# A fused attention, MLP and expert kernel: the zero fills of the slot table get a small tile of their own and a slot in the plan each, and the rows of expert 0 are loaded later in the load queue

## The chip, the cores and the metric

The kernel runs on one core of one Trainium2 chip. The metric is device time in microseconds (us) of one execution; lower is better. The median of three executions of the kernel before is 712.17 us (711.56 to 714.05). The trace comes from one more execution, taken by the hardware profiler. Its five engines are TensorE (PE; its weight loads are listed as PEld), VectorE (DVE), ScalarE (ACT), GpSimd (POOL) and SyncE (SP). SP and POOL both start DMA transfers; those of POOL are on a queue of their own.

## The reference, cut to what matters

```python
x = attention(q, k, v)          # 4 batches, 8 heads, 576 positions, window of 64
x = x.transpose(...).reshape(2304, 512)
h = x @ w_in                    # 512 -> 2048
g = h * tanh(softplus(h))
x = g @ w_out                   # 2048 -> 512
do_compute = x @ w_skip > 0     # tokens that go to an expert
e = argmax(x @ w_gate)          # one of 8 experts each, with its softmax weight
out = x;  out[do_compute] += gate * (relu(x @ w1[e]) @ w2[e])
```

## The kernel before, in words

**Slots.** The tokens are routed through a table in device memory, `xg_d`: 8 experts times 256 slots, 2,048 rows of 514 words (512 of the token, its gate, its token number). The row of a slot that no token takes must hold zeros and a token number out of bounds. So the kernel first fills the table (`fill_zero`, `fill_store`, tasks `fz` and `fs`), then scatters each routed token into its slot by an indirect DMA from POOL (`scatter`, tasks `sd`, lines 275 to 281), and later loads the rows of each expert (`base_load`, task `bl`, lines 1052 to 1056, for expert 0, whose last tokens are picked by matmuls; `xg_load` for the rest).

**Stages.** The first program part runs attention and the MLP over 6 blocks `m` of 384 tokens. Each block has 16 chunks of the hidden width. For chunk `c` = 16 m + f, `L1` (line 737) makes the pre-activation in a PSUM tile `ph` (ring of 2), a chain on ACT and DVE (`mn` L742, `me`, `n`, `ln`, `r` on ACT, `g` L764, `gH`, `gL` L773) makes the activation, and `L2` (line 788) adds the chunk to three output tiles `po`. Attention for the next block (`S`, `mx`, `ex`, `nm`, `PT`, `Pe`, `PV`, by pairs of heads `pr`) runs between the chunks. After 16 chunks `x_evac` (`xe`, lines 826 to 834) copies each `po` into a tile `xs`, routing works on it, and the scatter sends it. The second program part runs the 8 experts.

**Weights.** In block 0 the weights of `L2` are whole float32 words (`w_f32`). From block 1 on they are split in two halves: `wide_back` (`wb`, line 681) copies `w_f32` by a DMA on SP into a `ca` tile, `wide_H` (`wH`, line 314/316) rounds it, and `wide_L` (`wL`, line 697) takes the remainder. There are 16 such copies. The `ca` tiles are a ring of 2. Expert weights come near the end of the first part through staging tiles `st` in the ring `cv` of 2 (`expert_load`, line 330; `expert_H`, line 314/316; `expert_L`, line 340, on POOL or DVE).

**Order.** A planner (class `Plan`) orders all tasks before the program is written. It simulates a clock with an assumed cost for each task, waits for the tasks named in `after` plus a latency `lat`, for a free buffer of each ring in `get`, and for the earliest start `t0`; among the ready tasks it takes the one due first. The program is emitted in that order. On the chip each engine runs its own instructions in that order and waits only for data and buffers. Nothing of the planner's clock is left in the program. `chunk_time(c)` is the planner's time of chunk c: 32.22 + 5.11 for each of the first 16 chunks + 4.4 for each later one, so 93.5 for chunk 12, 118.4 for 17, 122.8 for 18 and 131.6 for 20.

The zero tile `zt` of the kernel before is one of the three `xs` tiles: `xsp.tile([128, XW], F32, tag="xs", name="zt")`. It is in use until all 16 stores of it are done. POOL also writes small pads into tiles that SP loads, at the place of their load task: zeros in `rk` (line 475, with the load `lqk` of a pair) and in `vt` (line 400, with the load `lv`), and the token numbers into `xs` (line 834, with `xe`). Such a pad waits until the buffer is free.

Of the kernel before, what the change touches and what calls it, by code (L numbers as in the profile page):

```python
# [9 lines left out]
F32 = mybir.dt.float32  # L10
F32R = mybir.dt.float32r
BF16 = mybir.dt.bfloat16
I32 = mybir.dt.int32
# [7 lines left out]
BIG = 65536.0  # L21
CAP = 256
# [7 lines left out]
GAP, FILL = 0.15, 0.8  # L30
E2B = 0.3
X0 = 2.6
PRICE3 = dict(P=0, V=0.0, A=0.12, G=0.2, S=0)
AHEAD = 18
EARLY = 8
# [134 lines left out]
def tile_kernel(  # L170
# [14 lines left out]
    V, A, G, PE, SP = nc.vector, nc.scalar, nc.gpsimd, nc.tensor, nc.sync  # L185
    B, H, S, D = q.shape
    NT, DM = out.shape
    DFF = w_in.shape[1]
    NE, _, F2 = w1.shape
# [5 lines left out]
    XW = DM + 2  # L195
# [4 lines left out]
    xg_d = dram.tile([NE * CAP, XW], F32, name="xg_d")  # L200
# [4 lines left out]
    xsp = wst.enter_context(tc.tile_pool(name="xsp", bufs=3))  # L205
    xtp = wst.enter_context(tc.tile_pool(name="xtp", bufs=2))

    def ctile(shape, dt, name):
        return cst.tile(shape, dt, tag=name, name=name)
# [8 lines left out]
    for p0 in (0, 64):  # L218
        sl = maskA[p0:p0 + 64]
# [33 lines left out]
    for n in (1, 1, 1, 3):  # L253
        t = ctile([128, n, NE + 1], F32, f"first{len(first_t)}")
# [11 lines left out]
    def fill_tile(zt):  # L266
        V.memset(zt[:, :DM + 1], 0.0)
        V.memset(zt[:, DM + 1:XW].bitcast(I32), int(BIG))

    def fill_store(zt, n):  # L270
        G.dma_start(out=xg_d[128 * n:128 * n + 128, :], in_=zt)
# [91 lines left out]
    T = plan.add  # L363
    VV, AA, GG, PP, SS = ("V", V), ("A", A), ("G", G), ("P", PE), ("S", SP)

    def one(eng, cost):
        return [(eng[0], eng[1], cost)]
# [7 lines left out]
    def chunk_time(c):  # L375
        m, f = divmod(c, NF)
        return T0 + (min(c, NF) * D0 + max(c - NF, 0) * D1)
# [203 lines left out]
    for pr in range(NU // 2):  # L581
        t = unit_time(2 * pr) - 5
        if pr < NPE:
            T(("lqk", pr), one(SS, 2.62 if len(runs(pr // 4)) == 1 else 5.2), lambda e, pr=pr: load_nat(pr), lat=2.3,
              get=[("rk", ("nq", pr)), ("rk", ("nk", pr))], due=t, t0=.7)
            for i in (1, 0):
                T(("nT", pr, i), one(PP, .36), lambda e, pr=pr, i=i: nat_T(pr, i), after=[("lqk", pr)] + ([("S", pr - 1)] if pr else []),
                  get=[(f"po{i}" if pr < 4 else "ps", ("tqk", pr, i))], use=[("nq", pr) if i == 0 else ("nk", pr)])
        else:
            T(("lqk", pr), one(SS, 3.6 if len(runs(pr // 4)) == 1 else 7.2), lambda e, pr=pr: load_dvt(pr), lat=2.3,  # L590
              get=[("rq", ("nq", pr)), ("rk", ("nk", pr))], due=t - 5)
        nd = sum(3 if r[3] == 0 else 2 for r in runs(pr // 4))
        T(("lv", pr), [("S", SP, .53 * nd)], lambda e, pr=pr: load_v(pr, e), lat=2.3,
          get=[("vt", ("vt", pr))], due=unit_time(2 * pr))
    for pr in range(NU // 2):
        if pr < NPE:
            T(("kT", pr), two(.52, .6), lambda e, pr=pr: nat_k(e, pr), after=[("nT", pr, 1)],
              get=[("kT", ("kT", pr))], use=[("tqk", pr, 1)], behind=[("kT", pr - 1)] * (pr > 0))
            T(("qT", pr), two(.42, .52), lambda e, pr=pr: nat_q(e, pr), after=[("nT", pr, 0)],
              get=[("qT", ("qT", pr))], use=[("tqk", pr, 0)], behind=[("qT", pr - 1)] * (pr > 0))  # L600
            pre = [("kT", pr), ("qT", pr)]
        else:
            T(("qT", pr), one(VV, 1.0), lambda e, pr=pr: dve_T(pr), after=[("lqk", pr)],
              get=[("kT", ("kT", pr)), ("qT", ("qT", pr))], use=[("nq", pr), ("nk", pr)],
# [4 lines left out]
          after=pre + ([("PT", 2 * pr + j - DEEP) for j in range(2)] if early and 2 * pr >= DEEP else []) + ([] if early else [("PT", 2 * pr - 1)]),  # L609
          get=[("ph" if early else "ps", ("sc", 2 * pr + j)) for j in range(2)],  # L610
          use=[("kT", pr), ("qT", pr)], due=unit_time(2 * pr), behind=[("S", pr - 1)] * (pr > 0))
        for j in range(2):
            u = 2 * pr + j
            T(("mx", u), one(VV, .64), lambda e, u=u: att_max(u), after=[("S", pr)], get=[("u" if u in EXTRA else "P", ("P", u))],
              use=[("sc", u)])
# [3 lines left out]
        for j in range(2):  # L619
# [3 lines left out]
              get=[("ps", ("tp", u))],  # L623
              use=[("P", u)])
            T(("Pe", u), two(.38, .47), lambda e, u=u: att_PTe(e, u), after=[("PT", u)], get=[("PT", ("PT", u))],
              use=[("tp", u)])
        T(("PV", pr), one(PP, .9), lambda e, pr=pr: att_PV(pr), after=[("Pe", 2 * pr), ("Pe", 2 * pr + 1), ("lv", pr)],
          get=[("ps", ("pv", pr))], use=[("PT", 2 * pr), ("PT", 2 * pr + 1), ("vt", pr)])
        T(("xH", pr), two(.37, .47), lambda e, pr=pr: att_xH(e, pr), after=[("PV", pr)], use=[("pv", pr)],
          get=[("xHL", ("xHL", pr // 4))] if pr % 4 == 0 else (), behind=[("xH", pr - 1)] * (pr > 0))  # L630
        if pr // 4 < WHOLE["in"]:
            continue
        T(("xL", pr), one(VV, .47), lambda e, pr=pr: att_xL(pr), after=[("xH", pr)], use=[("pv", pr)],
          due=unit_time(2 * pr) + 10)
# [64 lines left out]
    for f in range(NF):  # L699
        for kind in ("in", "out"):  # L700
# [12 lines left out]
            if n:  # L713
# [4 lines left out]
              use=[ca])  # L718
# [247 lines left out]
        def scatter(self, t):  # L966
            scatter(xs_t[self.m, self.t0 + t], self.si[:, t])

    zt = [None]

    def fill_zero():
        zt[0] = xsp.tile([128, XW], F32, tag="xs", name="zt")
        fill_tile(zt[0])

    T(("fz",), one(VV, .55), lambda e: fill_zero(), get=[("xs", "zt")], due=chunk_time(17), t0=chunk_time(17))
    for n in range(NE * CAP // 128):
        T(("fs", n), one(GG, 1.04), lambda e, n=n: fill_store(zt[0], n), after=[("fz",)], use=["zt"],
          lat=6, due=chunk_time(18) + 1.0 * n)
    T(("wg",), one(SS, 1.0), lambda e: load_wgs(), due=chunk_time(2), lat=3)

    def load_wgs():
# [4 lines left out]
    for m in range(NB):  # L986
        last = m == NB - 1
        tb = chunk_time(NC) - 8 if last else chunk_time(NF * m + NF + 2)
        dt = 0.5 if last else D1
        for t in range(3):  # L990
            T(("xe", m, t), two(.48, .6), lambda e, m=m, t=t: x_evac(e, m, t), after=[("L2t", NF * m + NF - 1, t) if last else ("L2", NF * m + NF - 1)],
              get=[("xs", ("xs", m, t))], use=[("po", m, t)], due=tb + 2)
            T(("xo", m, t), one(SS, .45), lambda e, m=m, t=t: x_store(m, t), after=[("xe", m, t)], lat=2.5,
              due=tb + 20, use=[("xs", m, t)])
            T(("rT", m, t), one(PP, .43), lambda e, m=m, t=t: route_T(m, t), after=[("xe", m, t)] + [("re", m, t - 1)] * (t > 0),
              get=[("ps", ("rtp", m, t))], due=tb + dt * (2 + 2 * t), use=[("xs", m, t)])
            T(("re", m, t), two(.48, .6), lambda e, m=m, t=t: route_Te(e, m, t), after=[("rT", m, t)],
              get=[("rk" if last else "xf", ("xf", m, t))], use=[("rtp", m, t)])
            if not last:
                T(("rl", m, t), one(PP, .25), lambda e, m=m, t=t: route_few(m, t), after=[("re", m, t), ("wg",)],  # L1000
                  get=[("ps", ("lq", m, t))], use=[("xf", m, t)], due=tb + dt * (3 + 2 * t))
                T(("rq", m, t), two(.22, .19), lambda e, m=m, t=t: route_fewe(e, m, t), after=[("rl", m, t)],
                  use=[("lq", m, t)], get=[("lqs", ("lqs", m))] if t == 0 else ())
                continue
            T(("rl", m, t), one(PP, .75), lambda e, m=m, t=t: route_lg(m, t), after=[("re", m, t), ("wg",)],
              get=[("ps", ("lp", m, t))], use=[("xf", m, t)], due=tb + dt * (3 + 2 * t))
        if not last:
            T(("rs", m), one(PP, .66), lambda e, m=m: route_sum(m), after=[("rq", m, t) for t in range(3)],
              get=[("ps", ("lp", m))], use=[("lqs", m)], due=tb + dt * 8.5)
            T(("lg", m), one(VV, .1), lambda e, m=m: route_lge(m), after=[("rs", m)], use=[("lp", m)])  # L1010
        prev = None
        for t0, n in ([(t, 1) for t in range(3)] if last else [(0, 3)]):
            g = Group(m, t0, n)
            lgs = [("lg", m) if n > 1 else ("rl", m, t0)]
            lu = [("lp", m, t0)] if n == 1 else []
            key = lambda x, m=m, t0=t0: (x, m, t0)
            td = tb + dt * 9
            gb = ("grp", m, t0)

            def R(name, eng, cost, fn, after, use=(), late=0.0, get=(), lat=None, g=g, gb=gb, td=td):  # L1020
                T(name if isinstance(name, tuple) else key(name), one(eng, cost), lambda e: fn(g), after=after,
                  use=[gb] + list(use), due=td + late, get=get, lat=lat)

            T(key("m1"), one(VV, .1), lambda e, g=g: g.max1(), after=lgs, use=lu, get=[(f"grp{n}", gb)], due=td)
            R("dm", VV, .1, Group.dm, lgs + [key("m1")], lu)
            R("su", VV, .1, Group.sub, [key("m1")], lu)
            R("se", AA, .12, Group.exp, [key("su")])
            R("fi", VV, .1, Group.first, [key("su"), key("dm")])
            R("m2", VV, .1, Group.max2, [key("fi")])
            R("oh", VV, .1, Group.onehot, [key("m2")])  # L1030
            R("pl", PP, .1, Group.place, [key("oh")] + ([prev("co")] if prev else [("co", m - 1, 0)] if m else []),
              get=[("ps", ("pp", m, t0))])
            R("pi", VV, .1, Group.pick, [key("pl")], [("pp", m, t0)], .5)
            R("ro", VV, .1, Group.row, [key("pi")], (), .5)
            R("sl", VV, .07, Group.slot, [key("ro")], (), .5)
            R("ke", VV, .07, Group.keep, [key("ro")], (), .3 if last else 6)
            R("sm", VV, .1, Group.sum, [key("se")], (), .5)
            R("ep", VV, .07, Group.eps, [key("sm")], (), .5)
            R("ga", VV, .09, Group.gate, [key("ep")], (), .5)
            R("tg", VV, .07 * n, Group.tag, [key("ga")], [("xs", m, t0 + t) for t in range(n)], .5)  # L1040
            R("co", VV, .21 * n, Group.count, [key("pl")], (), 1)
            for t in range(n):
                R(("sd", m, t0 + t), GG, 1.04, lambda g, t=t: g.scatter(t),
                  [key("sl"), key("tg"), ("xo", m, t0 + t)] + [("fs", x) for x in range(NE * CAP // 128)],
                  [("xs", m, t0 + t)], 2, lat=3)
            prev = key


# [371 lines left out]
```

## Time and profile before

| | |
|---|---|
| median of 3 executions | 712.17 us (711.56 to 714.05) |
| the profiled execution | 712.69 us |
| its span, first to last instruction | 710.9 us |
| PE busy | 685.3 us (96%) |
| DVE, ACT, POOL busy | 444.2 (62%), 396.7 (56%), 76.8 us (11%) |
| mean granted TensorE clock | 0.986 of full speed |
| chain of work that ended last | PE 76%, issue 7%, DMA 6%, DVE 4%, ACT 2% |

The chain of work that ended last is followed back from the last instruction, at each step to what released it. In the timeline rows below, the columns are start (us), length (us), engine, source line, operation, output<-input, how many were merged, and in square brackets the idle time before it with what ended it. A row that merges several instructions has the length from the first start to the last end. 1.8 us of the execution lie outside the span.

### The profile page before, as it was taken

What the parts mean: (1) busy time and instruction counts of PE and PEld (TensorE: products, weight loads), DVE (VectorE), ACT (ScalarE), POOL (GpSimd) and SP (SyncE); (2) the same over time, 40 slices, a digit from 0 to 9 for tenths busy, and PEclk for the clock granted to TensorE, in tenths of its full rate; (3) what the DMA queues carried; (4) which work ended last, traced back from release to release, by engine and by line L of the source; (5) the groups of instructions that cost most, each with busy time, mean ns of one, the idle gap of its engine ahead of it and who ended that gap; (6) DMA issues with size and microseconds to landing.
All of it is one profiled execution on the core that took longest, in us unless ns stands there. A gap on an engine that the chain in (4) does not pass through costs nothing.

```text
span 710.9 us, 13617 instructions
## 1 busy us (share of the span) xinstructions
PE 685.3 (96%) x4921; PEld 584.8 (82%) x4921; DVE 444.2 (62%) x1247; ACT 396.7 (56%) x973; POOL 76.8 (11%) x144
## 2 busy tenths in 40 slices
PE   7999999889999999999999999999988999999994
PEld 7876667678888888888888888888878998998983
DVE  5899999486566657565467556446557362574251
ACT  6778877367656675766566666556643342232120
POOL 3000000400020001000020000112232111111011
PEclk9999999989999999999999999999998999999998
DMA  7789887943213213231221200054463667788000
GB/s 176 215 242 270 263 205 158 339 153 73 42 53 87 41 29 73 46 89 30 41 54 34 64 1 9 18 184 144 131 198 105 243 237 236 265 290 290 30 24 20
DMA packets 141644, 92.53 MB, mean 130 GB/s; under 512 B 110189, under 2 KB 118381, under 8 KB 141568
## 3 DMA queue, kind: packets, MB, share of 16 engines
q1 hardware_dynamic: 137568, 82.90, 40.3%
q0 software_dynamic: 4000, 8.63, 3.4%
q8 instruction: 45, 0.74, 0.4%
q14 instruction: 31, 0.25, 0.1%
HBM read 73.96 MB, written 17.86 MB: 129 GB/s over the span
## 4 chain that ended last, share of the span: by engine, by line
PE 76%; issue 7%; DMA 6%; DVE 4%; ACT 2%; SPq 2%; POOL 1%; POOLq 0%; DVEq 0%; ACTq 0%
PE po L788 27%; PE ph L737 26%; PE ph L1209 7%; PE po L1253 4%; PE sc L508 2%; PE pv L563 2%; DMA ca<-w 2%; DMA st<-in_moe_w_dram 2%; PE tp L552 2%; DMA w<-in_moe_w_in_dram 1%; PE rtp L843 1%; DMA vt<-in_v_dram 1%; PE po L1268 1%; PE lq L857 1%; POOL out_dram L291 1%
## 5 line engine op out<-in xcount | busy, mean ns | idle before, releaser
L737 PE MATMUL ph<-xH,w 128*128 128x384 f32 x768 | 223.3, 352 | 4.3 <-DVE u L764 3.0
L788 PE MATMUL po<-w,gH 128*128 128x512 f32 x480 | 154.7, 404 | 1.8 <-ACT xs L830 1.8
L737 PEld LDWEIGHTS ph<-xH,w 128*128 128x128 f32 x768 | 141.6, 189 | 13.4 <-issue 5.1
L737 PE MATMUL ph<-xL,w 128*128 128x384 f32 x384 | 130.5, 340 | 0.0
L788 PEld LDWEIGHTS po<-w,gH 128*128 128x128 f32 x480 | 89.3, 191 | 17.2 <-ACT xs L830 2.2
L745 ACT ACTIVATE u<-u 128x384 f32<-128x384 f32 x96 | 50.0, 521 | 94.7 <-DVE u L742 94.6
L788 PE MATMUL po<-w,gL 128*128 128x512 f32 x240 | 95.8, 399 | 0.0
L764 DVE SCALAR_TENSOR_TENSOR u<-u,ph 128x384 f32<-128x384 f32 x80 | 44.1, 552 | 75.1 <-ACT u L758 74.2
L737 PEld LDWEIGHTS ph<-xL,w 128*128 128x128 f32 x384 | 72.6, 189 | 2.2 <-issue 1.4
L742 DVE TENSOR_SCALAR u<-ph 128x384 f32<-128x384 f32 x96 | 53.0, 553 | 25.9 <-PE ph L737 25.7
L531 ACT ACTIVATE P<-P,mx 128x128 f32<-128x128 f32 x144 | 55.8, 389 | 16.2 <-DVE mx L524 16.1
L1209 PEld LDWEIGHTS ph<-xgT,w 128*128 128x128 f32 x512 | 63.7, 190 | 0.9 <-ACT xgT L314 0.3
L1209 PE MATMUL ph<-xgT,w 128*128 128x144 f32 x512 | 64.1, 286 | 0.2 <-ACT xgT L314 0.2
L788 PEld LDWEIGHTS po<-w,gL 128*128 128x128 f32 x240 | 45.7, 190 | 11.6 <-DVE gL L773 0.7
L749 ACT ACTIVATE u<-u 128x384 f32<-128x384 f32 x96 | 50.3, 523 | 2.7
L755 ACT ACTIVATE u<-u 128x384 f32<-128x384 f32 x96 | 50.2, 523 | 2.6
L758 ACT ACTIVATE u<-u 128x384 f32<-128x384 f32 x96 | 50.2, 523 | 2.5
L773 DVE TENSOR_TENSOR gL<-u,gH 128x384 fp32r<-128x384 f32 x80 | 46.5, 581 | 5.9 <-ACT gH L314 3.1
L1236 ACT ACTIVATE hH<-ph 128x288 fp32r<-128x288 f32 x32 | 13.1, 410 | 60.9 <-PE ph L1209 49.9
L788 PE MATMUL po<-w,g 128*128 128x512 f32 x96 | 44.4, 599 | 0.0
L1253 PE MATMUL po<-w,hH 128*128 128x512 f32 x128 | 42.6, 414 | 0.0
L276 POOL DMA_INDIRECT xg_d<-xs,r_si x18 | 18.4, 1023 | 166.2 <-DVE P L547 78.3
(159 smaller groups left out, 1002.3 us busy)
## 6 DMA issues: line engine op xcount, KB each, us to landing
st<-in_moe_w_dram SPq DMA_DIRECT2D x64, 256.0 KB, 5.9
w<-in_moe_w_dram SPq DMA_DIRECT2D x32, 512.0 KB, 5.6
w<-in_moe_w_in_dram SPq DMA_DIRECT2D x16, 512.0 KB, 6.1
w<-in_moe_w_out_dram SPq DMA_DIRECT2D x16, 512.0 KB, 6.1
out_dram<-xs SPq DMA_DIRECT2D x18, 256.0 KB, 2.2
xg_d<-zt POOLq DMA_DIRECT2D x16, 257.0 KB, 7.1
xg<-xg_d SPq DMA_DIRECT2D x16, 257.0 KB, 3.6
ca<-w SPq DMA_DIRECT2D x16, 256.0 KB, 2.4
```

The lines of the kernel that those rows point to most:

```text
L531: A.activation(P[:, i], P[:, i], AF.Exp, bias=mx[:, 0, u % 2, i:i + 1], scale=-1.0, accum_out=mx[:, 1, u % 2, i:i + 1])
L737: PE.matmul(phs[c], a[:, kk], b[:, kk], start=kk == 0 and n == 0, stop=kk == NK - 1 and n == len(terms) - 1)
L742: V.tensor_scalar(u, phs[c], 20.0, None, op0=ALU.min)
L745: A.activation(us[c], us[c], AF.Exp)
L749: A.activation(us[c], us[c], AF.Square, bias=1.0)
L755: A.activation(us[c], us[c], AF.Ln, scale=0.5, bias=half_t[c])
L758: A.activation(us[c], us[c], AF.Exp, scale=-1.0)
L764: V.scalar_tensor_tensor(o, us[c], 1.0, phs[c], op0=ALU.subtract, op1=ALU.mult)
L773: eng.tensor_tensor(gL, us[c], gH.bitcast(F32), op=ALU.subtract)
L788: PE.matmul(po[m, t], a[:, ts], b, start=f == 0 and n == 0, stop=f == NF - 1 and n == len(terms) - 1)
L1209: PE.matmul(ph[:, i], w1_t[e, kk][:, 128 * f:128 * f + 128], xgT[e][:, kk, :N1], start=kk == 0, stop=kk == NK - 1)
L1253: PE.matmul(po2[e, s], a[:, f, ss], b, start=f == 0 and n == 0, stop=f == 7 and n == 2)
```

## The change

The zero tile is now a constant tile `nothing` of 130 words on each partition (128 zeros, one more zero, one out-of-bounds number), filled at the planner's time of chunk 12. Each of 16 stores writes the 512 token words of 128 rows from it, the 128 zeros read four times. A 17th store writes the last two words of all 2,048 rows. The stores stand in the plan from chunk 20 on, 2.5 us apart. The ring of `xs` tiles no longer holds the zero tile. And the planner's latency of a scatter goes from 3 to 6.5 us; what comes after a scatter in the plan is the load of expert 0's rows.

```diff
+FILL_AT, FILL_BY = 20, 2.5
-    zt = [None]
+    nothing = ctile([128, 1, 130], F32, "nothing")
+    NS = NE * CAP // 128
     def fill_zero():
-        zt[0] = xsp.tile([128, XW], F32, tag="xs", name="zt")
-        fill_tile(zt[0])
-    T(("fz",), one(VV, .55), lambda e: fill_zero(), get=[("xs", "zt")], due=chunk_time(17), t0=chunk_time(17))
-    for n in range(NE * CAP // 128):
-        T(("fs", n), one(GG, 1.04), lambda e, n=n: fill_store(zt[0], n), after=[("fz",)], use=["zt"],
-          lat=6, due=chunk_time(18) + 1.0 * n)
+        V.memset(nothing[:, :, :129], 0.0)
+        V.memset(nothing[:, :, 129:].bitcast(I32), int(BIG))
+    def fill_slots(n):
+        if n < NS:
+            G.dma_start(out=xg_d[128 * n:128 * n + 128, :DM].rearrange("p (a c) -> p a c", c=128),
+                        in_=nothing[:, :, :128].to_broadcast([128, DM // 128, 128]))
+        else:
+            G.dma_start(out=xg_d.rearrange("(n p) c -> p n c", p=128)[:, :, DM:XW], in_=nothing[:, :, 128:].to_broadcast([128, NS, 2]))
+    T(("fz",), one(VV, .2), lambda e: fill_zero(), due=chunk_time(12), t0=chunk_time(12))
+    for n in range(NS + 1):
+        T(("fs", n), one(GG, 1.04), lambda e, n=n: fill_slots(n), after=[("fz",)],
+          lat=6, due=chunk_time(FILL_AT) + FILL_BY * n, t0=chunk_time(FILL_AT) + FILL_BY * n)
...
                 R(("sd", m, t0 + t), GG, 1.04, lambda g, t=t: g.scatter(t),
-                  [key("sl"), key("tg"), ("xo", m, t0 + t)] + [("fs", x) for x in range(NE * CAP // 128)],
-                  [("xs", m, t0 + t)], 2, lat=3)
+                  [key("sl"), key("tg"), ("xo", m, t0 + t)] + [("fs", x) for x in range(NS + 1)],
+                  [("xs", m, t0 + t)], 2, lat=6.5)
```

## Rows read from the trace of the kernel before

**Rows 1.** Waits of PE from 60 to 560 us: total, times, longest (us).

```profile
PE sel L1062 <- DVE u L764: 3.0, 1, 3.0
PE ph L737 <- DVE u L764: 3.0, 1, 3.0
PE po L788 <- ACT xs L830: 1.8, 1, 1.8
```

**Rows 2.** Timeline of PE, 128 to 165 us.

```profile
128.43 0.42 PE L737 MATMUL ph<-xH,w 128*128 128x384 f32 x1
...
136.45 0.89 PE L508 MATMUL sc<-kT,qT 64*64 64x128 f32 x24
...
140.37 0.44 PE L737 MATMUL ph<-xH,w 128*128 128x384 f32 x1 [3.03 <-DVE u L764]
...
152.39 0.34 PE L737 MATMUL ph<-xH,w 128*128 128x384 f32 x1
...
154.51 0.64 PE L788 MATMUL po<-w,gH 128*128 128x512 f32 x2
...
156.62 0.82 PE L552 MATMUL tp<-ident,P 128*128 128x128 f32 x6
```

**Rows 3.** Windows: us, busy us (instructions) by engine, granted clock, DMA share, GB/s.

```profile
100.00:123.00 23.00, 22.70 (x130) 15.57 (x128) 22.28 (x60) 17.24 (x46) 0.16 (x1) 1.00 0.70 153
130.41:154.70 24.29, 19.48 (x116) 15.60 (x115) 15.30 (x43) 11.03 (x30) 3.29 (x9) 0.86 0.81 258
535.00:540.00 5.00, 5.00 (x25) 4.40 (x25) 1.99 (x5) 1.14 (x3) 0.29 (x1) 0.78 0.40 150
```

**Rows 4.** Timeline of DVE, 125 to 140 us.

```profile
125.08 0.55 DVE L764 SCALAR_TENSOR_TENSOR g<-u,ph 128x384 f32<-128x384 f32 x1
...
135.28 0.43 DVE L316 CAST w<-ca 128x512 fp32r<-128x512 f32 x1 [4.87 <-DMA ca<-w]
...
137.76 0.43 DVE L316 CAST w<-ca 128x512 fp32r<-128x512 f32 x1 [1.58 <-DMA ca<-w]
```

**Rows 5.** DMA from 123 to 142 us: a queue, and issues with KB and landing.

```profile
q0 software_dynamic: 1280, 4.21, 62.2%
...
ca<-w SPq DMA_DIRECT2D x4, 256.0 KB, 6.2
```

**Rows 6.** DMA issues of the whole span: KB each, median us to landing.

```profile
ca<-w SPq DMA_DIRECT2D x16, 256.0 KB, 2.4
...
wgs<-in_moe_w_skip_dram SPq DMA_DIRECT2D x1, 2.0 KB, 5.8
```

**Rows 7.** Timeline of POOL, whole span.

```profile
109.25 0.16 POOL L475 MEMSET rk<- 128x64 f32 x1 [55.28 <-DVE kT L490]
123.28 5.04 POOL L271 DMA_DIRECT2D xg_d<-zt  x9 [13.87 <-DVE mx L538]
...
162.62 0.20 POOL L400 MEMSET vt<- 64x128 f32 x1 [19.95 <-PE pv L563]
...
521.77 1.32 POOL L340 TENSOR_TENSOR w<-st,w 128x512 fp32r<-128x512 f32 x1
```

**Rows 8.** Instructions on the tile zt: ns minimum, median, maximum, first and last start.

```profile
L271 POOL DMA_DIRECT2D xg_d<-zt x16: 539/539/757, 123.3 to 134.1; - x16
```

**Rows 9.** Timeline of SP: copies of weights, expert 0's rows, staging loads.

```profile
119.20 2.00 SPq L681 DMA_DIRECT2D ca<-w  x2
...
525.27 0.89 SPq L1056 DMA_DIRECT2D base<-xg_d  x2
...
526.25 0.85 SPq L330 DMA_DIRECT2D st<-in_moe_w_dram  x2
```

**Rows 10.** The chain that ended last, in order of time, 515 to 535 us.

```profile
520.69 4.37 DMA xg_d<-xs,r_si
```

**Rows 11.** Timeline of ACT, 522 to 558 us.

```profile
530.79 0.63 ACT L314 ACTIVATE w<-st 128x512 fp32r<-128x512 f32 x1 [6.59 <-DMA st<-in_moe_w_dram]
```

**Rows 12.** Instructions on the tile xs, 200 to 240 us.

```profile
L832 DVE TENSOR_SCALAR xs<-po x1: 692/692/692, 222.2 to 222.2; 128x512 f32<-128x512 f32 x1
```

## The prediction

> **What bounds the kernel now.** I read four views in turn. The chain that ended last names TensorE for most of the span, so only time in which PE waits or runs slowly can be won. The waits of PE before the experts are few: two of 3.0 us and one of 1.8 [rows 1] (each 3.0 is one event; an earlier list by line counts it for the weight load too). So I looked at what leads to these three.
>
> *First place, 137 to 152 us.* PE ends a score group at 136.45 + 0.89 = 137.34 and is back at full pace at 152.39, 15.05 us later [rows 2]. Between them it does one L1, two L2 and four transposes. At full pace an L1 takes 154.51 - 152.39 = 2.12, an L2 156.62 - 154.51 = 2.11, and six transposes 0.82, so four 0.55 [rows 2]: 6.9 us. Lost: 15.05 - 6.9 = 8.1. A second way gives the same: waits of 3.0 + 1.8, and a granted clock of 0.86 over 24.29 us, which is 3.4 [rows 1, 3]. The cause is upstream. DVE sat idle 4.87 and 1.58 us for copies of weights `ca` [rows 4]. These took 6.2 us from issue to landing between 123 and 142, against 2.4 over the whole span, and the queue of POOL filled 62.2% of all DMA time there [rows 5, 6]. That queue carried the 16 zero stores, issued from 123.28 on, the first nine in 5.04 us [rows 7]. The 1.8 wait is the third `xs` tile, whose buffer the zero tile held.
>
> *Second place, 525 to 540 us.* SP reaches the load of expert 0's rows and must wait for the scatters, which land at 520.69 + 4.37 = 525.06 [rows 10]. It issues it at 525.27; two staging loads queued behind it go out at 526.25 [rows 9]. ACT waits 6.59 us for the first and starts at 530.79 [rows 11]; the activation chain behind it on ACT is late, and PE waits 3.0 for the `ph` buffer [rows 1]. From 535 to 540 the granted clock is 0.78, another 5 x 0.22 = 1.1 [rows 3].
>
> **The change, part by part.**
>
> *The fills leave 123 to 142.* Worth at most the 8.1. It cannot all come back. In the stretch 130.41 to 154.70 DVE is busy 15.30 us [rows 3]; with 8.1 less the stretch is 16.2, so DVE would be 94% busy and in order. I give back 1.0 (bounds 0 and 2.0, twice that).
>
> *Where they go.* The 2.5 us between stores is in the planner's clock alone. On the chip POOL runs its queue as fast as its waits allow, and its waits are few. The zero tile is ready early (planner 93.5). The pad at 109.25, for the load of pair 12, is POOL's last work before the fills, and POOL then waits 13.87 us only because the zero tile is not there [rows 7]. That wait goes. What else stands between the fills in POOL's order are pads. Following the planner of the kernel before, the load of pair 13 is at 137.2 and the v load of pair 12 at 151.9 of its clock; the fills start at 131.6 + 2.5 n. So about three come before the first of these pads, six between the two, and eight after. The pad of pair 13 needs a buffer that DVE frees some us after 109, on the same order of work as the one at 109.25. The v pad waits for a PE step that ended at 162.5 [rows 7]. So I expect about nine fills in a batch from 110 us on, and the others, with the 17th, after about 162.6 - 7 = 155.5, when the 16 copies have nearly all been issued.
>
> *Price of the first batch.* It falls on a stretch where DMA is 0.70 and DVE 22.28 of 23 us busy [rows 3]; two copies go out on SP at 119.20 [rows 9], among many small loads. Below: nothing. Nine of 16 fills would make a copy late by 9/16 of 6.2 - 2.4, which is 2.1 [rows 5, 6], and the activation that ends at 125.08 + 0.55 = 125.63 has 2.8 us until PE needs its buffer at 128.43 [rows 2, 4]. Above: 9/16 of the old 8.1, 4.6, since a DVE with 3% idle cannot make up a late start. I take 2.0, nearer to the slack, because the copies then needed are few. Of the second batch I take 0 (bounds 0 and 1.0): PE has caught up and one or two copies are left.
>
> *Smaller pieces.* A store now moves 512 pieces of 512 bytes instead of 128 rows. POOL's time for one was 539 ns at the minimum and the median [rows 8]; the bounds are that and four times that, 2.2 us. Slower would only space the batch out: cost 0. The 17th store has 2,048 pieces of 8 bytes. The nearest row is a load of 512 words that took 5.8 us [rows 6]; four times that is 23 us. It lies under the time until the first scatter is needed, below. The fill of the small tile takes DVE a fraction of what it did; a tenth or so of a us either way, taken as 0.
>
> *The later load of expert 0's rows.* In the plan the load can start 3.5 us later, so the two staging loads go ahead of it. The first needs the staging buffer that POOL frees at 521.77 + 1.32 = 523.09 [rows 7]. It is issued 526.25 - 523.1 = 3.1 earlier, ACT starts at 527.7, and the wait of 3.0 and the slow clock, 1.1, go: 4.1. The next thing late is the last chunk, whose chain follows on the same ACT and DVE: I give back 0.7. Worth 3.4, bounds 0 and 4.1. The rows of expert 0 come no later than before, for the wait on the scatters (525.06) ends their delay in either order.
>
> **The sum** is made against the profiled execution, 712.69 us; the median of the runs, 712.17, is 0.5 lower, less than any term. 712.69 - 8.1 + 1.0 + 2.0 - 3.4 = 704.2. Between the three waits and up to 560 us PE has no others of weight [rows 1], so what is won stays won.
>
> **The rivals.**
>
> *Paced.* POOL takes so long for each store that they spread out, and the first batch costs nothing: 712.69 - 8.1 + 1.0 - 3.4 = 702.2. For it: four times the pieces. Against: nine stores took 5.04 us, 0.56 each, while DVE was fully at work [rows 4, 7]. The Trainium skill ("SBUF — State Buffer", section "SBUF: two separate sides") says that POOL cannot write the descriptors of its DMAs while VectorE holds the port pair that they share. By it the stores, moved into DVE's busiest stretch, would be drawn out and the time would be this rival's 702.2; the 0.56 of those rows does not bear it out.
>
> *Stall moved.* The first batch stalls the copies of 114 to 121 us as the old one did those of 127: all of the 8.1 is given back and 712.69 - 3.4 = 709.3 is left. For it: DVE has less slack there than at 130. Against: nine fills, not 16.
>
> *No gain in the second place*, because the staging load meets another wait: 704.2 + 3.4 = 707.6.
>
> *Slower: the 17th store holds up the scatters.* The second batch starts at 155.5. At 2.2 us each its seven large stores end on POOL at 170.6, the 17th (16 times 0.54) at 179.2 and has landed, at 23.2, at 202.4. Three scatters of some 1.3 and a landing of 4.4 [rows 10] end at 210.7. The first `xs` tile of block 1 is filled at 222.2 [rows 12], after the change at some 215. So it costs nothing until the 17th store takes more than 27.6 us; at twice my figure, 46.4, it is 18.8 late, PE stands still, and the time is 704.2 + 18.8 = 723. The Trainium skill ("DMA: Bandwidth & Descriptors", section "Specifications") says that pieces under 512 bytes make the DMA read, modify and write. It speaks for this rival at 723; no row here shows a store of 8 bytes.
>
> *Reordered.* The freed ring and the new due times shift the plan around the fills; a worse order in a stretch where DVE is full takes the gain back: 710 to 716.
>
> **Chances and range.** Forecast 704.2: 0.52, its own range 701.5 to 707. Paced 0.13, stall moved 0.14, no gain in the second place 0.07, slower 0.05, reordered 0.09, of which a third ends slower. By the bounds the best is 712.69 - 8.1 - 4.1 = 700.5; above I reach past the moved stall to 710.5. That leaves out the slower rival, most of the reordered one and tails of the others, some 2 in 10. A measurement of this kernel tells 0.3%, 2.1 us, from no change. Faster by more: 0.84; within: 0.08; slower: 0.08.
>
> **What would show it.** POOL's timeline: fills from 110 us in two or three batches, split by the pads; single fills 2.5 us apart would be the pacing rival. The windows from 130 to 155: granted clock back to 1.00, no wait of DVE for `ca` of more than 1 us. DMA: copies `ca` near 2.4 us at all times but 114 to 125. SP: the rows of expert 0 behind two staging loads, ACT at its staging wait 3 us earlier, and no 3 us wait at PE's first selection matmul. I am wrong if DVE waits for copies around 117 to 125 and PE loses over 4 us there, or if a scatter waits for the 17th store.

## The result, and the profile after

The changed kernel takes 717.25 us (median of 8 runs, 716.57 to 718.15) against 712.85 us for the kernel before (8 runs, 708.86 to 714.77). The ratio is 1.0065, with a 95% interval of 1.0043 to 1.0086: slower by 0.65%, where 704.2 us, 1.2% faster, was forecast. The profiled execution took 717.19 us, with a span of 715.5.

To see where the 4.6 us between the two spans (710.9 and 715.5) went, I cut both at the same four instructions: the zeroing of the pad `rk` at 109.25 [rows 7], the first zeroing of V's pad behind the scatters, the first matmul of the experts and the last delivery. The two that have no row yet are these. Of the kernel before, the timeline of POOL and of PE:

```profile
204.88 0.20 POOL L400 MEMSET vt<- 64x128 f32 x1 [4.47 <-PE pv L563]
...
702.81 0.98 POOL L291 DMA_INDIRECT out_dram<-y,xg  x1 [5.00 <-DVEq L1388]
```

```profile
554.19 6.03 PE L1209 MATMUL ph<-xgT,w 128*128 128x144 f32 x47 [0.19 <-ACT xgT L314]
```

and of the changed kernel the same two, POOL's with the fills that answer to [rows 7]:

```profile
110.56 0.16 POOL L476 MEMSET rk<- 128x64 f32 x1 [54.50 <-DVE kT L491]
...
111.14 0.99 POOL L980 DMA_DIRECT2D xg_d<-nothing  x1 [0.18 <-issue]
...
112.37 1.54 POOL L980 DMA_DIRECT2D xg_d<-nothing  x2
...
113.98 3.21 POOL L980 DMA_DIRECT2D xg_d<-nothing  x4
119.31 0.76 POOL L980 DMA_DIRECT2D xg_d<-nothing  x1 [2.12 <-DMA rq<-in_q_dram]
168.17 0.20 POOL L401 MEMSET vt<- 64x128 f32 x1 [48.10 <-PE pv L564]
168.73 2.98 POOL L980 DMA_DIRECT2D xg_d<-nothing  x4 [0.36 <-issue]
...
181.82 1.16 POOL L983 DMA_DIRECT2D xg_d<-nothing  x1 [7.04 <-issue]
...
211.52 0.20 POOL L401 MEMSET vt<- 64x128 f32 x1 [4.55 <-PE pv L564]
...
704.80 0.98 POOL L292 DMA_INDIRECT out_dram<-y,xg  x1 [4.52 <-DVEq L1398]
```

```profile
556.63 3.58 PE L1219 MATMUL ph<-xgT,w 128*128 128x144 f32 x27 [0.20 <-ACT xgT L315]
```

| stretch, us | before | after | difference | forecast |
|---|---|---|---|---|
| span's start to the pad `rk` | 109.25 | 110.56 | +1.3 | 0 |
| to V's pad: the first place | 95.6 | 101.0 | +5.3 | -5.1 |
| to the experts: the second place | 349.3 | 345.1 | -4.2 | -3.4 |
| to the last delivery | 148.6 | 148.2 | -0.4 | 0 |
| to the end of the span | 8.1 | 10.7 | +2.6 | 0 |

Each stretch is read from one trace of each kernel. In the ten traces of this document with the new fills, the changed kernel's among them, the work up to the pad `rk` is the same, and it takes 109.0 to 113.2 us; so the +1.3 of the first line says nothing.

The second place came out as forecast. The first is off by 10.4 us, and there is a loss at the very end that I had not looked for at all.

**The first place.** POOL did what was forecast: eight stores from 111 us on, in a batch, the others behind V's pad. The old stall of PE is gone, and with it the waits of 3.0 us at `ph` and 1.8 at `po` [rows 1], but there is a larger one that begins twelve microseconds earlier, at 125.4. Its row, the longest wait of PE from 60 to 565 us, and the windows view (as in [rows 3]) of the work behind it:

```profile
134.17 0.69 PE L738 MATMUL ph<-xH,w 128*128 128x384 f32 x1 [8.79 <-DVE g L765]
```

```profile
134.17:140.07 5.90, 5.90 (x15) 4.87 (x16) 3.43 (x9) 2.83 (x6) 0.00 (x0) 0.50 0.66 157
```

So the loss has two parts. PE waits 8.8 us, and behind the wait it does 5.90 us of matmuls at a granted clock of 0.50, the lower of its two levels (1.2 GHz); at full clock these would take half, an estimate from the two levels, so 2.95 us go there. Waits of DVE from 100 to 200 us, as in [rows 1]:

```profile
DVE kT L491 <- DMA rk<-in_k_dram: 10.2, 1, 10.2
DVE w L317 <- DMA ca<-w: 7.9, 4, 6.0
```

DVE stands 10.2 us, up to 130.24, at the transpose of pair 10's keys, and PE behind it. Not a weight copy `ca` was late there but the loads of q and k. (The 6.0 us at a `ca` come later, at 177.87, behind the second batch of stores; PE then waits 0.68.) SP, which issues the loads, was itself held up. Its timeline, where most of these issues took some 0.47 us each up to 111 us:

```profile
111.36 0.42 SPq L482 DMA_DIRECT2D rk<-in_k_dram  x1
111.83 2.08 SPq L479 DMA_DIRECT2D rq<-in_q_dram  x1
...
115.59 1.21 SPq L479 DMA_DIRECT2D rq<-in_q_dram  x1
116.85 3.40 SPq L482 DMA_DIRECT2D rk<-in_k_dram  x1
120.36 8.46 SPq L411 DMA_DIRECT2D vt<-in_v_dram  x2
```

The DMA view of 110 to 130 us says with what they shared (queue: packets, MB, share of 16 engines' time; issues: KB each, median us to landing):

```profile
q0 software_dynamic: 640, 2.10, 59.1%
q1 hardware_dynamic: 6146, 1.31, 47.4%
...
xg_d<-nothing POOLq DMA_DIRECT2D x8, 256.0 KB, 9.4
...
rq<-in_q_dram SPq DMA_DIRECT2D x6, 48.0 KB, 9.4
```

Read the packets. On the mean, one of POOL's carries 2.10 MB / 640 = 3.3 KB and took 0.591 x 20 us x 16 / 640 = 0.30 us; one of SP's carries 1.31 MB / 6146 = 213 bytes. In the kernel before, POOL's packets carried as much (4.21 MB / 1280) and took 0.622 x 19 x 16 / 1280 = 0.148 us [rows 5]. So with 512-byte pieces in place of rows of 2,056 the same bytes took twice the packet time, and the packets of eight fills add up to 0.591 x 20 = 11.8 us of all sixteen engines, as those of all sixteen fills did before (0.622 x 19 = 11.8). The shares of the two queues here add up to more than 100%, so packets of different queues overlap in the record: a packet's time is not time in which its engine serves nothing else. The Trainium skill ("DMA: Bandwidth & Descriptors", section "Queues, rings and completion order") says that an engine goes round its queues by whole packets; by that a load of 128-byte pieces gives way to 3.3 KB each turn, and the landing of 9.4 us for 48 KB agrees.

**The second place.** SP issues the staging loads ahead of expert 0's rows, as was worked out from [rows 9], and ACT waits 1.42 us where it waited 6.59 [rows 11]:

```profile
528.91 2.67 SPq L331 DMA_DIRECT2D st<-in_moe_w_dram  x2
531.69 0.37 SPq L328 DMA_DIRECT2D w<-in_moe_w_dram  x1
532.36 0.88 SPq L1066 DMA_DIRECT2D base<-xg_d  x2
```

```profile
533.81 0.63 ACT L315 ACTIVATE w<-st 128x512 fp32r<-128x512 f32 x1 [1.42 <-PE ph L738]
```

The window that was at a granted clock of 0.78 [rows 3] is at full clock, and the first selection matmul does not wait:

```profile
535.00:540.00 5.00, 5.00 (x29) 4.12 (x28) 3.89 (x7) 3.57 (x8) 2.96 (x5) 1.00 0.53 173
```

**The end.** Behind the last delivery only sequencers work. POOL's last instructions belong to the closing of the program, and its longest drain (ns minimum, median, maximum) takes 2,282 ns where it took 731. First the kernel before, then the changed one:

```profile
L1415 POOLq DRAIN  x3: 44/103/731, 709.4 to 710.6; - x3
```

```profile
L1425 POOLq DRAIN  x3: 45/103/2282, 712.4 to 715.2; - x3
```

### The profile page after: what moved, and what is told of

It reads as the page before. It is cut to its first block, busy times and chain, and to the rows that moved or that the text cites. A ratio compares the mean times of both kernels' runs of the same rounds, so it can differ in the third digit from the quotient of the medians.

```text
span 715.5 us, 13609 instructions
## 1 busy us (share of the span) xinstructions
PE 684.6 (96%) x4921; PEld 583.3 (82%) x4921; DVE 444.1 (62%) x1245; ACT 397.8 (56%) x975; POOL 81.1 (11%) x145
## 5 line engine op out<-in xcount | busy, mean ns | idle before, releaser
L789 PE MATMUL po<-w,gH 128*128 128x512 f32 x480 | 152.9, 399 | 0.0
L746 ACT ACTIVATE u<-u 128x384 f32<-128x384 f32 x96 | 50.0, 521 | 89.7 <-DVE u L743 89.6
```

The costliest lines, as they stand in the source:

```text
L746: A.activation(us[c], us[c], AF.Exp)
L789: PE.matmul(po[m, t], a[:, ts], b, start=f == 0 and n == 0, stop=f == NF - 1 and n == len(terms) - 1)
```

## The experiments

In all of them the stretches of the table above are taken between the same instructions, again from one trace each. Where two kernels do the same in the first place, it differs by 0.7 us (95.6 in the kernel before, 94.9 with the later load alone) and by 1.3 (101.0 in the changed kernel, 102.3 with the fills alone). Theory A: the loss is DMA time that the early batch takes from pair 10's loads, and the second place is a separate gain. Its rivals: the loss comes from the order (the small tile is zeroed early, so the plan puts pair 10's transposes some 2.4 us earlier on DVE), or from the later load of expert 0's rows.

### One part of the change at a time

The kernel before with the later load alone:

```diff
-                  [("xs", m, t0 + t)], 2, lat=3)
+                  [("xs", m, t0 + t)], 2, lat=6.5)
```

> The kernel before with one number changed: a scatter is due to land 6.5 us after its issue instead of 3, so expert 0's rows go to the queue some 4 us later; the zero fills stay as before. Theory A (the two parts of the change are apart, and the second part gains where the forecast put it): the experts start about 4.2 us earlier than in the kernel before, and the time is 4.2 us under it, 0.9935 to 0.9950 of it. Rival (the later load's gain is given back after the last work, as the changed kernel's end, 2.2 us longer from the last delivery to the end of the span, suggests): 2.0 us under it, 0.997.

Measured: 708.86 us, 0.9938 of the kernel before (0.9910 to 0.9966). The stretch to the experts is 344.9 us against 349.3, the end 8.0. The later load is worth 4.5 us there, and nothing of it is lost at the end, so the longer end belongs to the fills.

The changed kernel without it:

```diff
-                  [("xs", m, t0 + t)], 2, lat=6.5)
+                  [("xs", m, t0 + t)], 2, lat=3)
```

> The changed kernel with the scatters' landing back at 3 us, so only the zero fills differ from the kernel before. Theory A (the batch of eight fills at 111 to 120 us costs 11.7 us against a first place without them, and 6.6 us against the kernel before): the time is 6.6 us over the kernel before, 1.008 to 1.011, and with the 2.2 us at the end, if that belongs to the fills, 1.012. Rival (the loss comes with the later load of expert 0's rows): within 0.3% of the kernel before.

Measured: 722.36 us, 1.0134 (1.0094 to 1.0174). First place 102.3 us (+6.7), second 348.4, end 10.3. The rival is out: the fills alone lose more than the whole change does, by about the 4.2 us that the other part gains.

### The same order without the early batch

In the changed kernel the stores 0 to 7 are issued where the ninth is; no other engine's order changes.

```diff
-FILL_AT, FILL_BY = 20, 2.5
+FILL_AT, FILL_BY, HOLD = 20, 2.5, 8
...
     def fill_slots(n):
+        if n < HOLD:
+            return
+        for x in range(HOLD) if n == HOLD else ():
+            fill_one(x)
+        fill_one(n)
+
+    def fill_one(n):
```

> The changed kernel with the order of every engine as it is and one difference: the first eight fills are issued together with the ninth, behind the zeroing of V's pad at 168 us, instead of at 111 to 120 us. Theory A (what was lost is DMA time: the eight fills starve pair 10's loads of q and k, and VectorE waits 10.2 us for them): that wait goes, the pads of V at 168.2 and 190.6 us come 11 to 14 us earlier, and the time is 703 to 706 us, 0.987 to 0.991 of the kernel before. Theory B (what was lost is the order: pair 10's transposes stand about 2.4 us earlier on VectorE because the small tile is zeroed early, and its loads are late with or without fills): a wait of at least 5 us stays at that transpose, and the time stays within 3 us of the changed kernel, 714 to 718 us.

Measured: 706.92 us, 0.9911 (0.9882 to 0.9941). The longest wait of PE that is left up to the experts is this:

```profile
PE ph L738 <- DVE u L765: 1.1, 1, 1.1
```

The granted clock is 1.00 from 110 to 155 us, and in the DMA view of 110 to 130 us the loads land as they should, though SP moves twice the bytes there:

```profile
q1 hardware_dynamic: 13619, 2.70, 66.1%
...
rq<-in_q_dram SPq DMA_DIRECT2D x12, 48.0 KB, 2.4
```

First place 89.7 us: 5.9 better than before, where the forecast had 5.1, and 11.3 better than the changed kernel. With the order as it was, this is theory A and against the rival of the order. The time is 1 us above the expectation; the end, 10.5 us, is still as long as in the changed kernel.

The sixteen stores now go out from 156.7 to 180 us in one row and land late (a median of 13.3 us from 155 to 182). What shares that stretch with them is late too. The loads of q and k there land in 19 us, against some 3 in the kernel before, and neither DVE nor PE waits for them: they are not needed yet. A weight copy lands late as well, and that one costs something, the price of the second batch that I had put at 0. First DVE, then PE:

```profile
166.26 0.43 DVE L317 CAST w<-ca 128x512 fp32r<-128x512 f32 x1 [6.38 <-DMA ca<-w]
```

```profile
167.93 0.44 PE L738 MATMUL ph<-xH,w 128*128 128x384 f32 x1 [1.11 <-DVE u L765]
```

### The whole row of fills later in the plan

The changed kernel with two numbers changed:

```diff
-FILL_AT, FILL_BY = 20, 2.5
+FILL_AT, FILL_BY = 25, 1.0
```

> The changed kernel with the fills planned from chunk 25 on, 1.0 us apart, instead of from chunk 20 on, 2.5 us apart: all seventeen stand behind two of the zeroings of V's and the keys' pads on POOL's queue and go out in a batch at about 155 to 172 us; SyncE's order is that of the changed kernel. Theory A: no wait for pair 10's loads, 703 to 706 us, 0.987 to 0.991 of the kernel before; a batch of seventeen there may delay what is loaded at 155 to 172 us, which would show as a VectorE wait there and cost up to the 5 us that the sixteen fills cost the kernel before. Theory B (order, not traffic): 714 to 718 us.

Measured: 707.06 us, 0.9913 (0.9882 to 0.9945). First place 90.5, second 345.4, end 10.6. The planner's own numbers do what the hold did by hand. The wait that was feared for the batch of seventeen is there, 7.2 us of DVE at a weight copy, but only 1.9 of it reach PE.

### The pace that was written, made real

In the changed kernel each store gets a small copy ahead of it that reads DVE's newest result; `recent` and the scratch tile `pace` are new:

```diff
     def m_L(eng, c):
         gH, gL = gHL[c]
+        recent[0] = gL
...
     def fill_slots(n):
+        G.tensor_copy(pace[:, n:n + 1], recent[0][:, :1].bitcast(F32))
```

> The changed kernel with a wait that paces GpSimd: in front of each of the seventeen stores it copies one column of the newest gL tile into a scratch tile, so that no store can leave before VectorE has made that gL; the order of every other engine is as in the changed kernel. Theory A (the loss is the batch at 111 to 120 us, which comes from GpSimd being ahead of the order's clock): no two stores start within 1 us of each other before 150 us, the first comes after 130 us, no VectorE wait for pair 10's loads over 1 us is left, and the time is that of the held fills, 0.988 to 0.994 of the kernel before. Rival (fills beside the loads of the attention cost what they cost, whenever they run): the waits come back a pair later, for pair 11's loads, 5 us or more, and the time is 0.997 or above.

Measured: 706.88 us, 0.9918 (0.9889 to 0.9947). Now POOL waits for DVE in front of a store, by its timeline:

```profile
130.91 0.32 POOL L981 COPY pace<-gL 128x1 f32<-128x1 f32 x1 [21.55 <-DVE gL L775]
131.17 0.99 POOL L983 DMA_DIRECT2D xg_d<-nothing  x1
...
136.00 0.18 POOL L981 COPY pace<-gL 128x1 f32<-128x1 f32 x1 [3.19 <-DVE gL L775]
136.12 0.79 POOL L983 DMA_DIRECT2D xg_d<-nothing  x1
136.90 0.20 POOL L981 COPY pace<-gL 128x1 f32<-128x1 f32 x1
137.02 0.75 POOL L983 DMA_DIRECT2D xg_d<-nothing  x1
```

The wait for pair 10's loads is gone. The pace is uneven: where a gL is already there, stores follow each other within 0.9 us, as at 136.12, so that detail of the expectation missed. PE pays 2.2 us at one gH, and the first place is 92.2 us, 2.5 worse than held; the end, 8.5 us, is 2.0 shorter. In time the two can't be told apart. The rival, a wait that returns for pair 11, did not appear.

### Half the batch

Four of the eight stay where they were; the diff is against the held kernel.

```diff
-FILL_AT, FILL_BY, HOLD = 20, 2.5, 8
+FILL_AT, FILL_BY, HOLD, NOW = 20, 2.5, 8, 4
...
-        if n < HOLD:
+        if NOW <= n < HOLD:
             return
-        for x in range(HOLD) if n == HOLD else ():
+        for x in range(NOW, HOLD) if n == HOLD else ():
```

> The changed kernel with four of the eight early fills left at 111 to 115 us and the other four held back to the ninth, behind the zeroing of V's pad. If the loss goes with the bytes that the fills put in front of pair 10's loads, VectorE's wait is about half of 10.2 us and the time about halfway between the held fills (0.991 of the kernel before) and the changed kernel (1.0065): 0.997 to 1.001. If the loads have slack for a few fills, the wait is under 1 us and the ratio 0.989 to 0.994. If the first fills alone make it, the wait stays 8 us or more and the ratio is 1.004 or more.

Measured: 710.98 us, 0.9984 (0.9962 to 1.0006). DVE's wait for pair 10's keys:

```profile
DVE kT L491 <- DMA rk<-in_k_dram: 4.5, 1, 4.5
```

No fills, four, eight: waits of 0, 4.5 and 10.2 us, first place 89.7, 94.1 and 101.0 us. DVE's wait is close to proportional, 1.1 to 1.4 us a store. In the first place the first four cost 4.4 us and the next four 6.9. The only slack seen is PE's, which is 1.4 us ahead of DVE and so waits 3.1 of the 4.5 and 8.8 of the 10.2; whether one or two stores would have fitted was not tried.

### Pieces of half the size

The changed kernel, with the early batch in its place:

```diff
-            G.dma_start(out=xg_d[128 * n:128 * n + 128, :DM].rearrange("p (a c) -> p a c", c=128),
-                        in_=nothing[:, :, :128].to_broadcast([128, DM // 128, 128]))
+            G.dma_start(out=xg_d[128 * n:128 * n + 128, :DM].rearrange("p (a c) -> p a c", c=64),
+                        in_=nothing[:, :, :64].to_broadcast([128, DM // 64, 64]))
```

> The changed kernel with each of the sixteen stores made of 1,024 pieces of 256 bytes instead of 512 pieces of 512 bytes: the same bytes at the same places of every queue, twice the pieces. If the loss in front of pair 10's loads goes with the bytes, VectorE's wait stays at 9 to 11 us and the ratio at 1.005 to 1.009; if it goes with the pieces, the wait is 15 to 20 us and the ratio 1.013 to 1.025. The end: if GpSimd's last drain goes with the pieces that it issued, the stretch from the last delivery's start to the end of the span is over 11.5 us; if it goes with the seventeenth store's 8-byte pieces alone, 10.3 to 10.7.

Measured: 734.54 us, 1.0296 (1.0271 to 1.0321). The time is above both expectations, but the wait for pair 10 is 9.6 us, not 15 to 20. The DMA view of 110 to 130 us says more:

```profile
q0 software_dynamic: 313, 1.03, 41.5%
```

Only half the bytes had gone by then, and they took 0.415 x 20 x 16 / 313 = 0.42 us a packet of the same 3.3 KB on the mean. POOL had to wait 7.89 us before its fourth store, and the rest ran on into the weight copies:

```profile
124.99 0.89 POOL L980 DMA_DIRECT2D xg_d<-nothing  x1 [7.89 <-issue]
```

```profile
DVE w L317 <- DMA ca<-w: 23.2, 4, 11.9
DVE kT L491 <- DMA rk<-in_k_dram: 9.6, 1, 9.6
```

So what counts is neither bytes nor stores alone. Counted in pieces that went out beside pair 10's loads, the three runs fall into line: 4 x 512 = 2,048 pieces and a wait of 4.5 us in the half batch, 8 x 512 = 4,096 and 10.2 us in the changed kernel, and here, up to 130 us, 1.03 MB / 256 = some 4,000 and 9.6 us. That is 2.2 to 2.5 us for each 1,000 pieces, from three runs; by that, the 8,192 pieces of all eight stores would have made some 18 to 20, as was expected, but they did not all go out in time.

The packets' times point the same way, less sharply: 0.148, 0.30 and 0.42 us a packet for pieces of 2,056, 512 and 256 bytes. These are times in a crowd, with other queues' packets between, and the crowd matters as much. At 512 bytes the DMA view gives 0.21 us in the paced run and 0.34 in the held one (both 155 to 182 us), at 256 bytes 0.34 here from 123 to 142. The Trainium skill ("DMA: Bandwidth & Descriptors", section "Specifications") puts the limit for full rate at 512 bytes; here a packet's time had already doubled at that limit, though not in the same crowd.

Two things are not told apart: the pieces' size, and that the new stores read the same few zeros over and over where the old ones read whole rows. The opposite run, rows of 2,056 bytes at the early place, was not tried.

### The end: which store it belongs to

Again against the held kernel:

```diff
-            G.dma_start(out=xg_d.rearrange("(n p) c -> p n c", p=128)[:, :, DM:XW], in_=nothing[:, :, 128:].to_broadcast([128, NS, 2]))
+            SP.dma_start(out=xg_d.rearrange("(n p) c -> p n c", p=128)[:, :, DM:XW], in_=nothing[:, :, 128:].to_broadcast([128, NS, 2]))
```

> The held fills with the seventeenth store (two words of every row, 2,048 pieces of 8 bytes) issued by SyncE instead of GpSimd. It is for the end of the program: from the last delivery's start to the end of the span the kernel before and the one with later rows alone take 8.1 and 8.0 us, every kernel with the new fills 10.3 to 10.7, with GpSimd's last drain at 2.28 us instead of 0.73. If the seventeenth store makes GpSimd's drain long, that stretch falls to 8.0 to 8.3 us and the time to about 0.988 of the kernel before; if the sixteen others do, it stays at 10.3 to 10.7 us and the ratio at 0.991.

Measured: 705.21 us, 0.9898 (0.9867 to 0.9930). POOL's longest drain falls to 894 ns, and SP issues the store in 0.47 us:

```profile
L1432 POOLq DRAIN  x3: 45/103/894, 701.6 to 703.1; - x3
```

The end is 8.8 us: 1.7 of the 2.4 us are back, less than expected. It is the seventeenth store on POOL that costs them, and not the sixteen others; in the run with twice their pieces the drain stayed at 2,282 ns and the end at 10.4 us. Which property of that store it is, its 2,048 pieces or their 8 bytes, was not tried.

Then the sixteen others as well:

```diff
-            G.dma_start(out=xg_d[128 * n:128 * n + 128, :DM].rearrange("p (a c) -> p a c", c=128),
+            SP.dma_start(out=xg_d[128 * n:128 * n + 128, :DM].rearrange("p (a c) -> p a c", c=128),
```

> The held fills with all seventeen stores issued by SyncE instead of GpSimd; nine stand in SyncE's order ahead of a wide copy and of pair 12's loads. The end: if what GpSimd issued makes its drain long, the stretch from the last delivery's start to the end of the span falls to 8.0 to 8.3 us; if not, it stays at 10.3 to 10.7. Beside it: if a store costs SyncE as much as its other issues near there (about 0.5 us), nothing is late and the time is 0.988; if the nine hold up SyncE by 1 us or more each, pair 12's loads are late, VectorE waits for them and the ratio is 0.993 or above.

Measured: 717.51 us, 1.0072 (1.0050 to 1.0094). The end is shorter than expected (6.6 us, with a longest drain of 1.13), but nine stores hold up SP for 9.60 us, and the weight copy and pair 12's loads stand behind them:

```profile
157.60 9.60 SPq L987 DMA_DIRECT2D xg_d<-nothing  x9
167.30 1.68 SPq L682 DMA_DIRECT2D ca<-w  x1
169.02 5.07 SPq L987 DMA_DIRECT2D xg_d<-nothing  x3
```

DVE waits 19.1 us at that copy and PE 13.9. The same stores on POOL's queue, at the same time, cost PE 1.1 us in the held run.

And the paced kernel with the seventeenth alone on SP:

```diff
-            G.dma_start(out=xg_d.rearrange("(n p) c -> p n c", p=128)[:, :, DM:XW], in_=nothing[:, :, 128:].to_broadcast([128, NS, 2]))
+            SP.dma_start(out=xg_d.rearrange("(n p) c -> p n c", p=128)[:, :, DM:XW], in_=nothing[:, :, 128:].to_broadcast([128, NS, 2]))
```

> The paced fills with the seventeenth store issued by SyncE. If the two gains are apart, the stretch at the end is 8.5 to 9.0 us and the ratio 0.988 to 0.991; if the pacing has cost in places that the other hid, it stays at 0.991 to 0.993.

Measured: 705.68 us, 0.9896 (0.9873 to 0.9920). The end is 6.8 us, shorter than expected, and again 1.7 us shorter than with the store on POOL (8.5). This and the held version with the last store on SP are the fastest; both beat both kernels.

One thing of the end stays open. Between the drain and the last delivery POOL pauses some 2 us longer in some kernels (the kernel before, the changed one, the held ones) than in others (the paced ones, and the one with all stores on SP: ends of 8.5, 6.8 and 6.6 us). It goes with the program and not with a wait that the trace shows; I did not try what sets it.

## Why the prediction was wrong

*The step that failed is the price of the first batch*: 2.0 us, with bounds of 0 and 4.6. Measured between the held and the changed kernel it is 101.0 - 89.7 = 11.3 us. It is made of the 8.8 us that PE waits and some 2.95 at the low clock behind it; the held kernel has 0.4 of these 11.7 at another place, for PE waits 1.11 us behind its second batch and 0.68 in the changed kernel. Three parts of the step were wrong. It scaled the old lateness by the number of stores, nine of sixteen, as if a store still weighed the same on the DMA engines; by the packets' times eight weighed as much as the old sixteen. It looked at the copies `ca` alone, which were named in the old wait, and not at the loads of q and k, of which SP issues eight for each pair, in pieces of 128 bytes, in the very stretch that the fills moved to. And its upper bound took the share of the old 8.1 us, which was the loss of a DVE with idle time around it (15.30 of 24.29 us busy); from 100 to 123 us DVE was busy 97% [rows 3], and of its wait of 10.2 us PE, which was 1.4 ahead, got 8.8. That the loads of q and k are what waits is shown by the held run. That a store weighs more in smaller pieces rests on the packets' times and on the run with half pieces. How much the third part adds was not measured apart. The rival that the stall moves had the right kind of mechanism, at 709.3 us, but named the copies; it was 8 us too small, 2.6 of them at the end.

*Smaller pieces* were priced on POOL, where they cost 0.75 to 0.99 us against 0.54, and the batch's own time indeed nothing. From 111.14 to 120.10 us DVE was busy 8.87 of 8.96 us; in the held kernel eight stores went out at 0.78 us each with DVE busy 2.18 of 6.32. The rule of the Trainium skill that I weighed ("SBUF — State Buffer", section "SBUF: two separate sides"), by which the stores would be drawn out while DVE holds the shared ports, is not borne out here either, though no trace shows when DVE holds them. The pieces were not priced on the DMA engines, and that was the error.

*The second batch* was taken as 0 with bounds of 0 and 1.0. PE waits 0.68 us behind it in the changed kernel, and 1.1 to 1.9 where all the stores stand there.

*The fills leave 123 to 142*: right in kind. Without the early batch the first place is 5.9 us better than before; the forecast with its 2.0 for the batch had 5.1, without it 7.1. So 2.2 of the 8.1 did not come back, where I gave back 1.0 for DVE; PE's wait behind the second batch is 1.1 of them.

*Where they go*: right. Eight, not nine, from 111.1 us on, the others behind V's pad; the planner's 2.5 us a store did not exist on the chip.

*The later load*: right, 4.2 against 3.4. The 0.7 given back was not lost; before it the gain was worked out at 4.1. The slow stretch of the kernel before ran from 533.9 to 537.3 us (granted clock 0.52), so its price was nearer 1.6 than the 1.1 read from the window that began at 535.

*The seventeenth store and the scatters*: right that it holds up nothing: issued in 1.16 us at 181.82, landed 7.6 us later, and the first scatter at 203.30 waits for DVE. Its real price was elsewhere: 1.7 us at the end, of which POOL's longest drain shows 1.4 (2,282 against 894 ns).

*Reordered*: the plan did shift, but the held kernel has the same order and shows no loss that would need it.

Put together: 704.2 + 10.4 (first place) - 0.8 (second) + 2.6 (the end) + 1.3 - 0.4 (the start, the experts) = 717.3, against 717.19 profiled.

## What to carry to other kernels

A planner's due time paces nothing: an engine with few waits runs its queue ahead, so ask of every moved store what really releases it, and if nothing does, put a real wait in front of it or stand it behind one. Price a DMA by its pieces and not by its bytes alone, and list every transfer that shares the stretch where it will run. Then ask of each of these how soon something waits for it: beside the early batch the loads of q and k landed in 9.4 us and cost PE 8.8, beside the held one they landed in 19 and cost nothing. And count the clock behind a long wait as part of its price. Look also at the end of the span, where a store of tiny pieces on POOL's queue is paid for in a drain.

## What the runs showed of the hardware

- A packet of zero stores, 3.3 KB on the mean, took 0.148 us with pieces of 2,056 bytes, 0.21 to 0.34 with 512 and 0.34 to 0.42 with 256, with packets of other queues under way beside it.
- Four and eight stores of 512 pieces, and some 4,000 pieces of 256 bytes, made a consumer of small loads wait 4.5, 10.2 and 9.6 us: 2.2 to 2.5 us for each 1,000 pieces.
- Beside such a queue SP's issue of a small load, 0.47 us otherwise, took up to 3.4 us in the changed kernel and 8.0 in the held one, and one pair of V loads 8.46 us for both.
- PE ran at a granted clock of 0.50 from 129.83 to 140.07 us after it had stood still from 125.38 to 134.17; in the held kernel, without that wait, the clock was 1.00 from 110 to 155.
- A store of 2,048 pieces of 8 bytes cost POOL 1.16 us to issue and 7.6 us to land, and left POOL's longest drain at the end of the program at 2.28 us instead of 0.89 with the store on SP, some 520 us after it had landed.
- Nine stores of 512 pieces cost SP 9.60 us; POOL issued eight of them in 6.24 us in the same place.
